# A new static order for one kernel: windowed attention and a channel mix on one core

## Chip, core and metric

One core of a Trainium2 chip. The metric is the device time of one execution in microseconds (us); lower is better. The engines are PE (TensorE: matmuls, with weight loads shown as PEld), DVE (VectorE), ACT (ScalarE), POOL (GpSimd) and SP (SyncE, which here issues nearly all DMAs).

## The reference

Attention over 4 batches of 8 heads, 768 positions and 64 dimensions, in which each position sees the 128 last positions and the first 4 (the sink), followed by a channel mix with three weight matrices:

```python
scores = scale * np.matmul(q, k.transpose(0, 1, 3, 2))
keep = (pos[None, :] < n_sink) | ((rel >= 0) & (rel < window))     # 4 and 128
a = softmax(np.where(keep, scores, -1e9))
x = np.matmul(a, v)                                  # heads side by side: (4, 768, 512)
xk = mu_k * x + (1 - mu_k) * x_prev                  # x_prev: one position earlier
xr = mu_r * x + (1 - mu_r) * x_prev
k = np.maximum(xk @ w_k, 0.0)                        # 512 -> 1024
out = sigmoid(xr @ w_r) * (k * k @ w_v)              # 1024 -> 512
```

All inputs and the output are float32 in HBM; the matmuls run in bf16.

## The kernel before

The work is cut into 12 units of 256 positions: unit u is third u % 3 of batch u // 3. A unit goes through these steps; the names are those of the tiles in the profile, the lines those of the kernel before.

- **Loads** (`load`, lines 284, 294 and 314; `load_weight`, line 330). Q, K and V of a unit come in two DMAs each, of 256 KB. For Q and K of the early units these are 256 pieces of 1 KB, for V (and for Q and K of later units) 1024 pieces of 256 bytes. W_k and W_v come in two DMAs of 1 MB each, W_r in one.
- **Casts to bf16**: `kb<-ks` and `qb<-qs` (lines 512 and 519), `vb<-vs` (617), and the weights `wk_sb`, `wr_sb`, `wv_h` (477, 481, 483).
- **Transposes** of K and Q: on PE into a PSUM bank (547) with a copy out to `kt` or `qt` (560), or, for K from unit 4 and Q from unit 8, by a DMA (534).
- **Attention** (`attend`): scores `sc` on PE (685), their exp `e` on ACT (739), the mask on DVE (753). The four sink positions have their own scores (660), exp `es` (667) and values (727). The value product (772) makes a bank from `e` and `vb`; the DVE takes a reciprocal (786) and writes `x` (789).
- **Mixing** (`mix`): `x` is transposed to `xt` (813, copied out at 822; in the last units by a DMA, 833), DVE forms the difference `td` (841) and eight products of line 852, four `xk` and four `xr`.
- **Channel mix** (`ffn`): key products on PE (903), relu `rl` on ACT or DVE (913, 917), its square `kk` on DVE (925), the gate product (934) with a tanh `th` on ACT (940), the value product `kk` times W_v in two half products (952), the output `ob` on DVE (961) and its store (968).

The order is not left to a run-time or compile-time scheduler. Every step is noted as an operation with a number by `Plan.op`. Three tables at the head of the file decide the rest: `CHOICE` names the engine of those casts, copies and relus that may run on more than one (ACT, DVE, for some POOL), `ORDER` is the one list in which all 1054 operations are emitted, and `SLOTS` gives the buffer of each tile. An engine runs its operations in the order of the list, one behind the other; a step whose operand is late holds up all behind it on its engine. A negative number in `ORDER` is a filler, a product of zeros on PE into a free bank (line 972).

```python
def run(self):
    keys = [(name, key) for o in self.ops for name, key in o["take"]]
    for (name, key), slot in zip(keys, SLOTS, strict=True):
        self.buf[key] = self.pools[name][slot]
    for i in ORDER:
        if i < 0:
            self.fill(self.pools["bank"][-1 - i])
        else:
            self.ops[i]["emit"]()
```

Four PSUM banks serve all products but the scores, which have two double banks of their own. Loads have three buffers each for K, Q, V and the 1 MB weight pieces.

Of the kernel before, what the change touches and what calls it, by code (L numbers as in the profile page):

```python
# [18 lines left out]
    90: "ACT", 92: "ACT", 94: "ACT", 98: "ACT", 100: "DVE", 103: "POOL", 106: "POOL", 111:  # L19
    "DVE", 112: "ACT", 113: "ACT", 139: "DVE", 142: "DVE", 145: "DVE", 148: "DVE", 152: "ACT",  # L20
    161: "DVE", 196: "DVE", 199: "POOL", 202: "DVE", 205: "ACT", 206: "ACT", 223: "DVE", 281:
    "POOL", 283: "DVE", 286: "DVE", 287: "ACT", 288: "DVE", 363: "DVE", 366: "ACT", 367: "ACT",
    438: "POOL", 446: "DVE", 447: "ACT", 449: "DVE", 456: "DVE", 516: "DVE", 518: "DVE", 521:
    "POOL", 526: "ACT", 527: "ACT", 547: "DVE", 605: "ACT", 606: "ACT", 679: "DVE", 684: "DVE",
    761: "ACT", 762: "ACT", 774: "DVE", 832: "DVE", 839: "ACT", 854: "DVE", 862: "DVE", 906:
    "POOL", 910: "DVE", 912: "DVE", 914: "ACT", 915: "ACT", 1004: "DVE", 1028: "DVE", 1036:
    "DVE",
# [15 lines left out]
PAIRS = ()  # L43

VS = ()
# [67 lines left out]
)  # L113

SLOTS = (
# [60 lines left out]
def kernel(  # L176
# [14 lines left out]
    nc = tc.nc  # L191
# [4 lines left out]
    NS = 4  # L196
# [9 lines left out]
    P = Plan()  # L206
# [820 lines left out]
```

## Time and profile before

| what | value |
|---|---|
| median of three runs | 170.79 us (169.55 to 171.17) |
| the profiled execution | 171.36 us |
| its span, first to last instruction | 169.6 us |
| granted TensorE clock | 0.999 |
| PE busy | 158.9 us (94%), 1569 instructions |
| DVE busy | 150.3 us (89%), 393 |
| ACT busy | 126.2 us (74%), 207 |
| POOL busy | 13.0 us (8%), 39 |
| read from HBM, written | 24.12 MB, 6.29 MB |

Busy time is summed per engine from first to last instruction; PE's includes the 32 fillers. A wait of an instruction is put down to the one that released it. Stretches are given in us from the first instruction.

### The profile page before, as it was taken

What the parts mean: (1) busy time and instruction counts of PE and PEld (TensorE: products, weight loads), DVE (VectorE), ACT (ScalarE), POOL (GpSimd) and SP (SyncE); (2) the same over time, 40 slices, a digit from 0 to 9 for tenths busy, and PEclk for the clock granted to TensorE, in tenths of its full rate; (3) what the DMA queues carried; (4) which work ended last, traced back from release to release, by engine and by line L of the source; (5) the groups of instructions that cost most, each with busy time, mean ns of one, the idle gap of its engine ahead of it and who ended that gap; (6) DMA issues with size and microseconds to landing.
All of it is one profiled execution on the core that took longest, in us unless ns stands there. A gap on an engine that the chain in (4) does not pass through costs nothing. (4 is left out here: it accounts for less than half of the span.)

```text
span 169.6 us, 4167 instructions
## 1 busy us (share of the span) xinstructions
PE 158.9 (94%) x1569; PEld 101.4 (60%) x1589; DVE 150.3 (89%) x393; ACT 126.2 (74%) x207; POOL 13.0 (8%) x39
## 2 busy tenths in 40 slices
PE   7997898969999999999999999999999999999991
PEld 2445476734657666767556686674665566664760
DVE  5159999699999999999999999999899999979851
ACT  4379998879997999799979998788658736731230
POOL 7520030001020001000000100000200000000000
PEclk9999999999999999999999999999999999999999
DMA  4999969999999999979969999999996761134303
GB/s 115 289 322 385 249 218 297 332 370 267 226 232 213 159 274 252 269 139 237 196 191 163 202 245 182 205 226 155 223 252 137 190 156 34 63 96 155 124 2 124
DMA packets 79043, 34.61 MB, mean 204 GB/s; under 512 B 67112, under 2 KB 73520, under 8 KB 79024
## 3 DMA queue, kind: packets, MB, share of 16 engines
q1 hardware_dynamic: 79008, 34.35, 87.0%
q8 instruction: 12, 0.20, 0.5%
q14 instruction: 7, 0.06, 0.1%
q10 hardware_dynamic: 16, 0.00, 0.0%
HBM read 24.12 MB, written 6.29 MB: 179 GB/s over the span
## 5 line engine op out<-in xcount | busy, mean ns | idle before, releaser
L903 PE MATMUL bank<-xk,wk_sb 128*128 128x256 bf16 x384 | 51.2, 273 | 0.9 <-DVE xk L852 0.4
L739 ACT ACTIVATE e<-sc 128x1024 bf16<-128x1024 f32 (+1 forms) x48 | 44.9, 961 | 1.7 <-PE sc L685 1.6
L952 PE MATMUL bank<-wv_h,kk 128*128 128x512 bf16 x173 | 44.7, 379 | 0.6
L903 PEld LDWEIGHTS <-wk_sb 128*128 128x128 bf16 x384 | 35.3, 98 | 10.4 <-issue 1.9
L913 ACT ACTIVATE rl<-bank 128x512 bf16<-128x512 f32 x41 | 24.0, 602 | 12.3 <-PE bank L903 7.9
L753 DVE TENSOR_TENSOR e<-e,mask 128x1024 bf16<-128x1024 bf16 (+1 forms) x48 | 30.2, 639 | 1.2 <-ACT e L739 1.0
L952 PEld LDWEIGHTS <-kk 128*128 128x128 bf16 x184 | 17.0, 98 | 16.0 <-DVE kk L925 0.3
L934 PE MATMUL bank<-wr_sb,xr 128*128 128x512 bf16 x87 | 23.5, 379 | 0.6 <-ACT rl L913 0.2
L852 DVE SCALAR_TENSOR_TENSOR xk<-td,mu_all,xt 128x256 bf16<-128x256 bf16 x48 | 22.2, 494 | 0.1
L852 DVE SCALAR_TENSOR_TENSOR xr<-td,mu_all,xt 128x256 bf16<-128x256 bf16 x48 | 22.2, 477 | 0.0
L940 ACT ACTIVATE th<-bank 128x512 f32<-128x512 f32 x24 | 14.5, 606 | 10.3 <-PE bank L934 8.8
L925 DVE TENSOR_TENSOR kk<-rl 128x512 bf16<-128x512 bf16 x48 | 19.4, 416 | 0.5 <-ACT rl L913 0.3
L789 DVE TENSOR_TENSOR x<-bank,rec 128x256 bf16<-128x256 f32 x48 | 19.5, 415 | 0.3
L772 PE MATMUL bank<-vb,e 128*128 128x65 bf16 x352 | 17.3, 194 | 2.3 <-DVE e L753 1.7
L772 PEld LDWEIGHTS <-e 128*128 128x128 bf16 x352 | 14.1, 97 | 6.6 <-DVE e L753 3.0
L961 DVE SCALAR_TENSOR_TENSOR ob<-th,bank 128x512 f32<-128x512 f32 x23 | 15.5, 678 | 1.2 <-PE bank L952 1.1
L934 PEld LDWEIGHTS <-xr 128*128 128x128 bf16 x96 | 9.1, 97 | 9.1 <-issue 0.7
L685 PE MATMUL sc<-qt,kt 64*128 64x128 bf16 (+1 forms) x256 | 13.8, 237 | 0.3 <-ACT kt L560 0.2
L617 ACT CAST vb<-vs 128x512 bf16<-128x512 f32 x18 | 11.3, 630 | 3.0 <-DMA vs<-in_v_dram 3.0
L685 PEld LDWEIGHTS <-kt 64*128 64x128 bf16 x256 | 9.2, 94 | 4.0 <-issue 2.1
L972 PE MATMUL bank<-warm 128*128 128x512 bf16 x32 | 10.1, 457 | 1.2 <-DVE warm L990 1.1
L841 DVE TENSOR_TENSOR td<-xt 128x512 bf16<-128x512 bf16 x24 | 10.0, 428 | 0.2
(71 smaller groups left out, 141.3 us busy)
## 6 DMA issues: line engine op xcount, KB each, us to landing
vs<-in_v_dram SPq DMA_DIRECT2D x24, 256.0 KB, 4.6
qs<-in_q_dram SPq DMA_DIRECT2D x24, 256.0 KB, 5.2
ks<-in_k_dram SPq DMA_DIRECT2D x24, 256.0 KB, 4.6
out_dram<-ob SPq DMA_DIRECT2D x23, 256.0 KB, 2.5
w<-in_moe_w_k_dram SPq DMA_DIRECT2D x2, 1024.0 KB, 9.1
w<-in_moe_w_v_dram SPq DMA_DIRECT2D x2, 1024.0 KB, 11.1
w<-in_moe_w_r_dram SPq DMA_DIRECT2D x1, 1024.0 KB, 7.8
kt<-kb SPq DMA_TRANSPOSE x16, 3.6
```

The costliest lines, as they stand in the source:

```text
L685: nc.tensor.matmul(out=sc[:, a, o0:o1], lhsT=lhs[rows], rhs=rhs[rows], start=u not in BIAS, stop=True, skip_group_check=u in BIAS)
L739: nc.scalar.activation(out=buf[ek][:, :, lo:], in_=buf[sck][:, :, lo:], func=AF.Exp, scale=scale)
L753: nc.vector.tensor_tensor(out=at, in0=at, in1=m, op=ALU.mult)
L772: nc.tensor.matmul(out=o[:, g, a, :], lhsT=e[:, a, e0:e0 + 128], rhs=rhs, start=(T == 0 and i == 0), stop=(i == len(blocks) - 1), skip_gro ...
L789: P.op("DVE", dve(256), lambda ok=ok, rk=rk, c=c: nc.vector.tensor_tensor(out=buf["x", u][:, :, 128 * c:128 * c + 128].rearrange("p g (a d ...
L852: nc.vector.scalar_tensor_tensor(out=buf[key][:, c, :], in0=buf[tk][:, i, :], scalar=mu[w][:, c:c + 1], in1=xt[:, c, t0 - 1:t0 + 255], op0 ...
L903: nc.tensor.matmul(out=ps[:, i, :], lhsT=wk_sb[:, c, 128 * f:128 * f + 128], rhs=xk[:, c, :], start=(c == 0), stop=(c == NC - 1), skip_gro ...
L913: nc.scalar.activation(out=buf[rk], in_=buf[psk].rearrange("p (i t) -> p i t", i=2), func=AF.Relu)
L925: P.op("DVE", dve(512, 0.52), lambda f2=f2, rk=rk: nc.vector.tensor_tensor(out=buf["kk", u][:, 2 * f2:2 * f2 + 2, :], in0=buf[rk], in1=buf ...
L934: nc.tensor.matmul(out=buf[psk], lhsT=buf["xr", u][:, c, 128 * g:128 * g + 128], rhs=wr_sb[:, c, :], start=(c == 0), stop=(c == NC - 1))
L952: nc.tensor.matmul(out=buf[psk], rhs=wv_h[:, f, :], lhsT=buf["kk", u][:, f, 128 * g:128 * g + 128], start=(f == 0), stop=(f == NF - 1))
L961: P.op("DVE", dve(512), lambda psk=psk, tk=tk, bk=bk: nc.vector.scalar_tensor_tensor(out=buf[bk], in0=buf[tk], scalar=1.0, in1=buf[psk], o ...
```

## The change

No operation is added or taken away. The three tables are replaced: 66 operations have another engine, `ORDER` and `SLOTS` are new. Code for two options that both stay empty (`ROWS4` and `BY_ACT`) is added and does nothing. The diff, cut to its core:

```diff
 CHOICE = {
-    90: "ACT", 92: "ACT", 94: "ACT", 98: "ACT", 100: "DVE", 103: "POOL", 106: "POOL", 111:
-    "DVE", 112: "ACT", 113: "ACT", 139: "DVE", 142: "DVE", 145: "DVE", 148: "DVE", 152: "ACT",
...
+    90: "ACT", 91: "ACT", 92: "ACT", 93: "ACT", 95: "ACT", 97: "ACT", 99: "ACT", 100: "POOL",
+    103: "POOL", 106: "DVE", 108: "DVE", 109: "DVE", 139: "POOL", 141: "DVE", 142: "DVE", 144:
...
+ROWS4 = ()
+
+BY_ACT = ()
...
 ORDER = (
-    78, 4, 80, 2, 87, 77, 81, 3, 83, 0, 1, 85, 112, 8, 9, 79, 82, 6, 86, 5, 84, 103, 109, -1,
-    -2, -3, -4, -1, -2, -3, -4, -1, -2, -3, -4, -1, -2, -3, -4, -1, 115, 7, 116, -2, 110, 104,
...
+    4, 79, 77, 80, 0, 78, 81, 1, 82, 85, 2, 3, 8, 83, 6, 7, 84, 112, 9, 86, 19, -1, -2, -3, -4,
+    -1, -2, -3, -4, -1, -2, -3, -4, -1, -2, -3, 115, 5, 100, -4, -2, -3, -4, -2, 101, 88, 102,
...
 SLOTS = (
...
```

What it comes to on each engine:

| operation | before: ACT, DVE, POOL | after: ACT, DVE, POOL |
|---|---|---|
| kb cast | 13, 6, 5 | 14, 5, 5 |
| qb cast | 14, 8, 2 | 11, 8, 5 |
| vb cast | 18, 3, 3 | 13, 5, 6 |
| kt copy | 7, 1, 0 | 6, 2, 0 |
| qt copy | 14, 2, 0 | 15, 1, 0 |
| xt copy | 14, 4, 0 | 15, 3, 0 |
| relu | 41, 7, 0 | 43, 5, 0 |
| W_k, W_r, W_v casts | 4, 6, 0 | 7, 3, 0 |

PE has the same products, with 44 fillers for 32.

**SP's first loads** (unit in figures, halves a and b; q and k halves are 256 KB):

- before: v0a q0a q0b k0a k0b q1a q1b k1a v0b k1b q2a q2b W_k-a W_k-b v1a v1b k2a k2b W_r v2a W_v-a v2b W_v-b q3a k3a q3b k3b q4a q4b k4a v3a q5a v3b k4b
- after: v0a k0a k0b q0a q0b q1a k1a k1b q1b q2a v0b q2b W_k-a k2a W_k-b k2b v1a v1b v2a W_r W_v-b W_v-a v2b q3a k3a k3b q3b q4a q4b q5a q5b k4a v3a v3b k4b

From the 39th of its 132 issues to the 118th the order is the same; of the last fourteen, some stores come earlier.

**POOL's first steps**, after the change: identity, head mask (`hmask`), first window mask (`mask0`), `spread`, vb of unit 0 (first half), sink column, kb and qb of unit 0, kb of unit 1 (first half), vb of unit 0 (second half), window mask, kb of unit 1 (second half), qb of unit 2. Before: window mask, `mask0`, `hmask`, identity, sink column, `spread`, qb and kb of unit 0, sink keys.

**ACT**, from its first copy out of PSUM:

- before: qt0 kt0 kt0 e0 e0 vb0 qt1 e0 e0 kt1 qt1 xt0 e1 e1 kt1 qt2 W_k(0) e1 es1 e1 qt2 rl0 vb1 rl0 W_k(2) kb2 xt1 kt2 xt1
- after: kt0 qt0 e0 qt0 e0 qb1 e0 e0 qb2 qt1 kt1 e1 e1 W_k(1) qt2 qt2 W_k(0) W_k(3) e1 vb1 es1 vb1 e1 rl0 rl0 W_k(2) xt1 kt2 xt1

**DVE** after the change has no cast of W_k any more (it had two); it takes W_r's first half at about the place where W_r's second half stood, and W_v's pieces 2 and 0 behind the two masks of unit 2's first pair, with a V cast of unit 2 between them. From unit 3 on, steps of an engine shift by two to five places on average against each other.

**ACT's first operation** is the small exp that brings the function table; the two DMAs of mu that ACT issues (line 350) come after it and not before.

More of the change, by code (lines that the diff above doesn't have):

```diff
@@ L18 @@
 CHOICE = {
-    90: "ACT", 92: "ACT", 94: "ACT", 98: "ACT", 100: "DVE", 103: "POOL", 106: "POOL", 111:
-    "DVE", 112: "ACT", 113: "ACT", 139: "DVE", 142: "DVE", 145: "DVE", 148: "DVE", 152: "ACT",
[L21 to L27, printed above, removed]
+    90: "ACT", 91: "ACT", 92: "ACT", 93: "ACT", 95: "ACT", 97: "ACT", 99: "ACT", 100: "POOL",
+    103: "POOL", 106: "DVE", 108: "DVE", 109: "DVE", 139: "POOL", 141: "DVE", 142: "DVE", 144:
+    "DVE", 145: "POOL", 151: "ACT", 152: "ACT", 154: "DVE", 161: "DVE", 193: "DVE", 196: "POOL",
+    199: "POOL", 205: "ACT", 206: "DVE", 223: "DVE", 284: "POOL", 287: "DVE", 288: "DVE", 320:
+    "DVE", 363: "DVE", 366: "ACT", 367: "DVE", 438: "DVE", 441: "POOL", 443: "POOL", 447: "ACT",
+    526: "DVE", 527: "ACT", 559: "DVE", 595: "DVE", 602: "DVE", 605: "ACT", 606: "ACT", 677:
+    "DVE", 681: "POOL", 683: "ACT", 684: "ACT", 753: "DVE", 774: "DVE", 830: "DVE", 832: "DVE",
+    838: "ACT", 839: "ACT", 854: "DVE", 908: "DVE", 914: "ACT", 1032: "DVE",
 }
@@ L262, in halves, with walked, block @@
         return slice(2 * half, 2 * half + 2) if u in PAIRS else slice(half, None, 2)
+    def walked(name, u):
+        return name in ROWS4 and by_dma(name, u)
+    def block(name, u, c, g=None):
+        t = buf[name + "t", u]
+        if not walked(name, u):
+            return t[:, c, :, :] if g is None else t[:, c, g, :]
+        t = t.rearrange("p c g t -> p (c g t)").rearrange(
+            "p (h j t w) -> p h w t j", h=2, j=4, w=2)[:, c % 2, c // 2]
+        return t if g is None else t[:, 32 * g:32 * g + 32]
     def by_dma(name, u):
@@ L283, in load @@
                     s0 = 256 * T + 128 * g
-                    P.op("SP", 600.0, lambda key=key, g=g, s0=s0: nc.sync.dma_start(
+                    queue, by = (nc.scalar, "ACT") if f"v{u}" in BY_ACT else (nc.sync, "SP")
+                    P.op(by, 600.0, lambda queue=queue, key=key, g=g, s0=s0: queue.dma_start(
                         out=buf[key][:, g, :, :],
@@ L290, in load @@
             src = {"k": k, "q": q}[name]
-            if by_dma(name, u):
+            if by_dma(name, u) and name not in ROWS4:
                 for g in range(2):
@@ L329, in load_weight @@
         key = ("w32", name, i)
-        P.op("SP", 600.0, lambda: nc.sync.dma_start(out=buf[key], in_=src), rank,
+        queue, by = (nc.scalar, "ACT") if what in BY_ACT else (nc.sync, "SP")
+        P.op(by, 600.0, lambda: queue.dma_start(out=buf[key], in_=src), rank,
              service=2930.0, descs=660, take=[("w32", key)], writes=[(name + "32", i)])
@@ L510, in cast @@
             def cast(copy, raw=raw, rk=rk, hs=hs, half=half, name=name):
-                if by_dma(name, u):
+                if by_dma(name, u) and name not in ROWS4:
                     return lambda: copy(
@@ L528, in prepare @@
                  hold=[raw] + ([rk] if half else []),
-                 reads=([(name, u, half)] if by_dma(name, u) or u in PAIRS else
+                 reads=([(name, u, half)] if by_dma(name, u) and name not in ROWS4 or u in PAIRS else
                         [(name, u, half, w) for w in range(2)]) + ["table"],
@@ L533, in prepare, with turn @@
             if by_dma(name, u):
-                P.op("SP", 1240.0, lambda key=key, rk=rk, half=half: nc.sync.dma_start_transpose(
-                    out=buf[key][:, :, half, :],
-                    in_=buf[rk][:, half, :, :].rearrange("p h d -> p (h d)")), rank + half,
+                def turn(key=key, rk=rk, half=half, name=name):
+                    to = buf[key][:, :, half, :] if name not in ROWS4 else buf[key].rearrange(
+                        "p c g t -> p (c g t)")[:, 512 * half:512 * half + 512].rearrange(
+                            "p (j m) -> p j m", j=4)
+                    nc.sync.dma_start_transpose(
+                        out=to, in_=buf[rk][:, half, :, :].rearrange("p h d -> p (h d)"))
+                P.op("SP", 1240.0, turn, rank + half,
                     service=930.0, descs=512, lag=1300.0, room=1200, reads=[rk + (half,)],
@@ L628, in prepare, with first @@
             return
+        def first(rows):
+            t = buf["kt", u]
+            if not walked("k", u):
+                return t[rows, :, 0, 0:NS]
+            return t.rearrange("p c g t -> p (c g t)").rearrange(
+                "p (h j t w) -> p (w h) t j", h=2, j=4, w=2)[rows, :, 0, :]
         def sink_keys():
@@ L634, in sink_keys @@
                 nc.gpsimd.tensor_copy(out=kz[rows, :, 4 * a:4 * a + NS],
-                                      in_=buf["kt", u][rows, :, 0, 0:NS])
+                                      in_=first(rows))
         P.op("POOL", 500.0, sink_keys, rank + 4, hold=[("kt", u)], port=True,
@@ L661, in sink_scores @@
                                          lhsT=ksink[b % 2][:, 32 * c:32 * c + 32],
-                                         rhs=buf["qt", w][:, c, :, :], start=True, stop=True)
+                                         rhs=block("q", w, c), start=True, stop=True)
             P.op("PE", 150.0 + 109.0 * (len(us) - 1), sink_scores, rank, lag=PE_LAG, mode=2,
@@ L676, in scores @@
             c = chunk(u, k)
-            kt, qt, sc = buf["kt", u], buf["qt", u], buf["sc", u, k]
-            jobs = [(kt[:, c, 0, :], 128, 384, qt[:, c, :, :]),
-                    (kt[:, c, 1, :], 384, 512, qt[:, c, 1, :])]
+            sc = buf["sc", u, k]
+            jobs = [(block("k", u, c, 0), 128, 384, block("q", u, c)),
+                    (block("k", u, c, 1), 384, 512, block("q", u, c, 1))]
             if T > 0:
-                jobs.append((buf["kt", u - 1][:, c, 1, :], 0, 128, qt[:, c, 0, :]))
+                jobs.append((block("k", u - 1, c, 1), 0, 128, block("q", u, c, 0)))
             for (lhs, o0, o1, rhs) in jobs:
@@ L696, in made @@
         def made(name, w, c):
-            if by_dma(name[0], w):
+            if by_dma(name[0], w) and name[0] not in ROWS4:
                 return [(name, w, 0), (name, w, 1)]
```

158 rows, old and new, of tables (ORDER, SLOTS) are left out of this document.

## The prediction

> **What bounds the kernel now.** First the page, for the shares and the DMA row:
>
> ```profile
> span 169.6 us, 4167 instructions
> ...
> PE 158.9 (94%) x1569; PEld 101.4 (60%) x1589; DVE 150.3 (89%) x393; ACT 126.2 (74%) x207; POOL 13.0 (8%) x39
> ...
> DMA  4999969999999999979969999999996761134303
> ```
>
> PE is the bound on the whole, with DVE close behind. A share is a mean over stages, so next the busy times by stretch (PE, PEld, DVE, ACT, POOL, each with its count, then clock, DMA share, GB/s):
>
> ```profile
> 10.00:20.00 10.00, 8.21 (x112) 5.05 (x109) 8.68 (x26) 9.88 (x17) 0.38 (x2) 1.00 1.11 343
> 20.00:30.00 10.00, 9.05 (x109) 6.29 (x109) 9.77 (x27) 9.53 (x17) 1.57 (x2) 1.00 0.81 242
> 30.00:40.00 10.00, 8.29 (x77) 5.45 (x78) 7.95 (x20) 8.14 (x14) 0.00 (x0) 1.00 1.08 346
> 40.00:60.00 20.00, 19.70 (x195) 12.18 (x197) 19.43 (x50) 18.95 (x35) 1.74 (x4) 1.00 1.03 209
> 60.00:110.00 50.00, 49.46 (x551) 33.31 (x558) 49.17 (x130) 45.38 (x75) 1.99 (x6) 1.00 1.08 214
> 110.00:160.00 50.00, 49.59 (x457) 31.71 (x463) 47.63 (x123) 29.17 (x46) 1.22 (x2) 1.00 0.68 147
> ```
>
> From 40 to 160 us PE idles 0.30 + 0.54 + 0.41 = 1.25 us in 120: no order can win more than that there. From 10 to 30 ACT is full. From 30 to 40 all three engines idle about 2 us, so something outside them ends last. The waits of the stretch 18 to 45 us name it, and SyncE's own timeline shows where it comes from:
>
> ```profile
> DVE wv_h L481 <- DMA w<-in_moe_w_v_dram: 1.9, 1, 1.9
> ...
> ACT vb L617 <- DMA vs<-in_v_dram: 1.2, 2, 0.8
> ...
> PE bank L772 <- DVE e L753: 0.9, 1, 0.9
> ```
>
> ```profile
> 10.97 5.53 SPq L284 DMA_DIRECT2D vs<-in_v_dram  x2
> 16.54 5.16 SPq L314 DMA_DIRECT2D ks<-in_k_dram  x2
> ...
> 24.34 2.31 SPq L284 DMA_DIRECT2D vs<-in_v_dram  x1
> 26.76 3.16 SPq L330 DMA_DIRECT2D w<-in_moe_w_v_dram  x1
> ```
>
> An issue takes about 0.6 us here; these took up to 4.8, because loads of V before them had filled the queue. After the second V load of unit 1, K of unit 2 was only accepted at 21.04 us. In the trace's landing times the fastest DMA engine finished that V load at 20.81 and the K load at 23.07, 2.26 us apart where loads of that size follow each other by 0.72 to 0.75: a hole of 1.5 us in the transfers (242 GB/s between 20 and 30 us, 343 before). It makes W_v late, DVE stands at its cast, and the mask of unit 2 behind it keeps PE's value product.
>
> **The change, part by part.** Times are of the profiled execution, 171.36 us: span 169.6 and 1.76 around it. It lies 0.57 above the median of the three runs, 170.79.
>
> *Work moved between engines.* 66 of the casts, copies and relus change engine. By the rows' means DVE loses a net 1 kb (0.42), 1 qt (0.68), 2 relus (1.37), 2 W_k and 1 W_v casts (1.37 + 0.69), 1 xt (0.42) and gains 1 kt (0.69), 2 vb (0.85): 3.4 us less of 150.3. ACT nets +0.6 us, but early: its two more W_k casts are 1.08 each. POOL gets 6 more casts of 0.61 to 0.94.
>
> *What a POOL cast costs DVE.* One td beside a POOL cast took longer than its group's mean of 428 ns:
>
> ```profile
> 41.02 0.67 POOL L519 CAST kb<-ks 128x512 bf16<-128x512 f32 x1 [15.57 <-DMA ks<-in_k_dram]
> ...
> 41.34 0.63 DVE L841 TENSOR_TENSOR td<-xt 128x512 bf16<-128x512 bf16 x1
> ```
>
> That is +0.20. Two products of line 852 beside the POOL cast at 49.44 took 1.23 us, where the pair at 35.53 took 0.88: +0.35. Six casts: 1.2 to 2.1 us, so DVE nets -1.3 to -2.2; I take -1.7. The rule that speaks against this part is in the Trainium skill, SBUF — State Buffer, "SBUF: two separate sides": the port pair of VectorE and GpSimd is an exclusive lock, and the loser blocks for the whole instruction. The trace shows delays on both sides, smaller than a whole cast on DVE's; the rule's own result is the third rival.
>
> *Start, to the first scores.* K of unit 0 is loaded ahead of Q, so it takes Q's landings (5.09 and 5.78 us) and Q takes K's (7.14, 8.73). POOL does its five set-up steps without the window mask (about 4.3 us from 1.28), one V cast and then the K cast, to about 7.0; the Q cast follows at 7.8, transposes (0.24) and ACT's copy (0.59) bring the first scores to about 8.9, from 10.37: 1.5 us earlier.
>
> *Unit 0's values.* The second half of V goes from ninth load to eleventh, landing at about 13.6 (what landed in that slot) instead of 12.13. Its cast moves to POOL (0.62), so the first value product starts at about 14.3, from 12.69: the 1.5 us are gone. Queued behind that cast on POOL are the window mask (0.54) and K's second half of unit 1, ready at about 15.8, from 13.94. On DVE the way from the first reciprocal (13.86 before) to unit 0's last xk (20.50) was 6.64 us; two Q casts (0.73) and a mask (0.62) leave it, one xt copy (0.42) joins, and 0.5 is lost to the late transposes: 5.7 + 0.5 from 14.8 gives 21.0, half a us late.
>
> *Unit 1's exps on ACT.* Between its first kt/qt copy and unit 1's last exp, ACT has six more steps of about 0.5 (start to start) and two W_k casts of 0.95, and five fewer of 0.5: +2.4. It starts 0.5 earlier. Its waits for a landing or for PE were 1.2 us; now it waits for scores, Q's last halves, K's transpose and V of unit 1, which I add up to 2.1. So the last exp ends at 22.22 + 1.9 + 0.9 = 25.0. Behind it are six steps (3.5 us) instead of nine (5.4) up to unit 1's last xt copy: 28.5, from 27.66. With the same 1.9 us of DVE work after it, the last xk of unit 1 is ready at 30.4, from 29.58, and the key products of unit 1 start +0.9 us late. The ends of this term: -0.5 (a third of the early scores survives) and +2.4 (ACT's whole added work is paid). I take +0.9; ACT idles only 0.12 of 10 us in that stretch, so its work passes through.
>
> *The loads of 20 to 38 us.* K of unit 2 now goes ahead of V of unit 1, between the halves of W_k, so the queue holds short loads when the V loads block, and the 1.5 us hole should close. W_r lands at about 28.1 (29.57), W_v's halves at 32.3 and 35.4 (34.16 and 37.89, order swapped), V of unit 2 last at 36.4 (35.17). PE then: key products of unit 1 (8 x 0.43) to 33.85, two gates (1.73) to 35.6, sink values and scores (0.77) to 36.35, a wait for V's cast on DVE to 36.85, two value products (0.5), a gate, half a product, a gate (2.6), a transpose (0.24), half a product (0.86): 41.05. Before, the same work (one half product for one gate) ended at 40.78 + 0.87 = 41.65. Net 0.6 us ahead, so this term alone is -1.5. Its ends: 0 (V of unit 2 or W_v is as late as before) and -1.7 (all of PE's idle in 30 to 40).
>
> *40 us to the end.* SyncE's order is unchanged from its 39th issue to its 118th; PE's and DVE's steps shift by two to five places on average. PE idles 1.25 us there, DVE 3.8, and DVE's work falls by about 1.2 after the start. Ends: -1.0 and +1.5 (a new order can add waits where there were none; the largest single one of DVE on PE was 0.9). I take -0.3.
>
> *Warm-up products.* 32 become 44, all before the first key product, in PE's waits (it idled 1.8 us between 10 and 20 us besides the fillers): nothing, and at most a filler's 0.22 when an operand arrives behind one.
>
> **Sum:** +0.9 - 1.5 - 0.3 = -0.9: 170.46 for an execution like the profiled one, 169.9 for the median.
>
> **Rivals.**
> 1. *The early scores carry through.* If V's late half does not hold unit 0 back by its full 1.5 us, the first term is -0.5; with the hole closed (-1.5) and -0.5 after: 170.79 - 2.5 = 168.3. For it: first scores 1.5 us early. Against: ACT is full from 10 to 30.
> 2. *Slower: V of unit 1 blocks ACT.* On ACT the two casts of unit 1's V now stand ahead of the sink exp and the last exp (before, one was on POOL and the other behind both). If that V lands 1.5 us later than the 23 us I count on, both exps, unit 1's values and its xk wait: the first term is +2.4, and the loads, late too, give back only 0.5: 172.7. It decides from a landing of about 24.5. For it: before, ACT waited 1.2 us for V. Against: nothing else stands between W_k and V than K of unit 2 (1.4 us).
> 3. *POOL takes what DVE gained.* If DVE is blocked for a whole cast (0.65), six cost 3.9 against 3.4 saved: DVE +0.5 and the last term +0.5 instead of -0.3: 170.7. Only two rows bear on it, and both show half or less. It is the Trainium skill's rule above, carried out.
> 4. *New waits after 40 us* of 2 us or more: 172.5. PE's idle of 1.25 leaves little trace of such waits now, but every order after 40 us is new.
>
> **How the numbers follow.** Forecast 0.45 (its own range 169.1 to 171.3), early scores 0.24, V blocks ACT 0.14, POOL 0.09, new waits 0.08. A measurement here can tell about 1% from no change, 169.1 to 172.5. Faster by over 1%: 0.24 and a few hundredths of the forecast, 0.27. Slower: 0.14 and half of 0.08, and a little of POOL, 0.20. Same: 0.53. The range goes to the low rival and the slow one: 168.0 to 172.7.
>
> **What would show it.** Right: first exp near 9, first value product near 14.3, no issue of K behind a V load longer than 2 us, DVE's wait for W_v gone, PE busy in 30 to 40 us above 9. Wrong: last exp of unit 1 before 23 or after 26.5; more than 2 us of PE idle from 40 to 160 us.

## The result, and the profile after

| | before | after |
|---|---|---|
| median | 170.11 us (168.92 to 172.31, 10 runs) | 172.28 us (170.98 to 174.07, 10 runs) |
| the profiled execution | 171.36 us | 171.27 us |

The ratio is 1.011 [1.0076, 1.0145]: slower by about 1.9 us, where 0.9 us less was forecast. (Ratios leave disturbed runs out, so they can differ from the quotient of two medians.) The two profiled executions don't show it: before's lies 1.25 us above its median, after's 1.0 below its own. What follows therefore uses several executions of each start.

The page of after, the lines that answer to those shown of before:

```profile
span 169.5 us, 4191 instructions
...
PE 159.6 (94%) x1583; PEld 102.3 (60%) x1601; DVE 148.3 (88%) x388; ACT 126.0 (74%) x206; POOL 18.5 (11%) x45
...
DMA  4999989999989998979995999999996894122303
```

DVE has 2.0 us less work and POOL 5.5 more. Busy times by stretch of after (PE, PEld, DVE, ACT, POOL, each with its count, then clock, DMA share, GB/s):

```profile
10.00:20.00 10.00, 8.85 (x117) 5.77 (x116) 8.34 (x23) 9.19 (x15) 3.73 (x8) 1.00 1.10 353
20.00:30.00 10.00, 8.75 (x110) 5.76 (x108) 9.58 (x26) 9.56 (x16) 1.10 (x1) 1.00 0.98 263
30.00:40.00 10.00, 9.85 (x90) 6.43 (x92) 9.96 (x25) 10.00 (x16) 0.61 (x1) 1.00 1.08 341
40.00:60.00 20.00, 19.83 (x200) 12.36 (x201) 19.58 (x51) 19.17 (x36) 1.88 (x5) 1.00 1.06 208
60.00:110.00 50.00, 48.64 (x549) 33.36 (x554) 47.44 (x128) 43.87 (x74) 2.79 (x5) 1.00 1.05 207
110.00:160.00 50.00, 49.02 (x457) 31.46 (x462) 46.61 (x118) 29.74 (x49) 2.11 (x4) 1.00 0.75 154
```

The idle time of 30 to 40 us is gone, on all three engines. From 40 to 160 us PE idles 0.17 + 1.36 + 0.98 = 2.5 us instead of 1.25. Before 20 us PE's busy time holds twelve more fillers, so a higher figure there is not more progress. The longest waits of after from 18 to 45 us, and SyncE's timeline:

```profile
POOL qb L535 <- DMA qs<-in_q_dram: 18.8, 2, 16.0
POOL kb L535 <- DMA ks<-in_k_dram: 5.6, 1, 5.6
PEld L755 <- issue: 1.2, 3, 0.4
PEld L931 <- ACT wk_sb L493: 0.9, 2, 0.7
```

```profile
10.20 1.30 SPq L329 DMA_DIRECT2D ks<-in_k_dram  x1
...
12.36 1.47 SPq L329 DMA_DIRECT2D ks<-in_k_dram  x1
13.88 7.97 SPq L299 DMA_DIRECT2D vs<-in_v_dram  x3
21.89 0.78 SPq L346 DMA_DIRECT2D w<-in_moe_w_r_dram  x1
22.79 5.03 SPq L346 DMA_DIRECT2D w<-in_moe_w_v_dram  x2
```

No wait of DVE or ACT for W_v or V is left, and no issue of K takes longer than 1.47 us. In this execution the loads did what was predicted. The start of after, from the timeline (start, length, instruction, idle time before it):

```profile
7.89 0.43 DVE L535 CAST qb<-qs 128x512 bf16<-128x512 f32 x1 [4.47 <-DMA qs<-in_q_dram]
7.92 0.87 POOL L535 CAST qb<-qs 128x512 bf16<-128x512 f32 x1 [0.88 <-DMA qs<-in_q_dram]
...
8.17 1.25 PE L1000 MATMUL bank<-warm 128*128 128x512 bf16 x5
...
8.23 0.83 DVE L535 CAST kb<-ks 128x512 bf16<-128x512 f32 x1
...
9.26 0.39 PE L568 MATMUL bank<-ident,qb 128*128 128x128 bf16 x4
9.48 0.81 PE L1000 MATMUL bank<-warm 128*128 128x512 bf16 x3
9.68 0.59 ACT L581 COPY qt<-bank 128x512 bf16<-128x512 bf16 x1 [0.98 <-PE bank L568]
...
10.32 0.51 PE L713 MATMUL sc<-qt,kt 64*128 64x256 bf16 x8
```

The first scores start at 10.32 us, not at 8.9: K is early, but Q's cast on POOL ends at 8.79, five fillers (L1000) are still ahead of its transposes at 9.26, and three more precede the scores.

Where the executions stand, in us. "First value product" and "unit u" are taken at a first weight load, that of the value products and that of unit u's key products; W_v is the landing of the half that comes first and of the one that comes last.

| execution | first value product | unit 0 | unit 1 | unit 2 | from 1 to 2 | W_v | its time |
|---|---|---|---|---|---|---|---|
| before | 12.69 | 20.16 | 28.51 | 51.42 | 22.91 | 34.16, 37.89 | 171.36 |
| before_again | 12.72 | 20.19 | 28.66 | 50.69 | 22.03 | 33.54, 37.29 | 171.33 |
| after | 13.87 | 21.47 | 30.48 | 50.43 | 19.95 | 32.16, 35.00 | 171.27 |
| after_again | 14.35 | 21.95 | 30.96 | 50.90 | 19.94 | 32.70, 36.33 | 171.93 |

So the new start is 1.8 to 2.5 us late when unit 1's key products begin, and in these executions wins 2.1 to 3.0 back by unit 2. The two executions of before are slow ones for their kernel: two other old starts below (old_to_63, old_k2_early), whose medians equal before's, begin unit 2 at 49.47 and 49.73.

### The profile page after: what moved, and what is told of

Read it like the earlier page. It is cut to its first block, busy times and chain, and to the rows that moved or that the text cites. A ratio compares the mean times of both kernels' runs of the same rounds, so it can differ in the third digit from the quotient of the medians.

```text
span 169.5 us, 4191 instructions
## 1 busy us (share of the span) xinstructions
PE 159.6 (94%) x1583; PEld 102.3 (60%) x1601; DVE 148.3 (88%) x388; ACT 126.0 (74%) x206; POOL 18.5 (11%) x45
## 4 chain that ended last, share of the span: by engine, by line
PE 59%; ACT 15%; DMA 11%; DVE 10%; issue 2%; SPq 1%; DVEq 0%; ACTq 0%
PE bank L931 16%; PE bank L980 16%; PE bank L962 8%; DMA ks<-in_k_dram 6%; PE bank L1000 5%; PE bank L800 4%; ACT e L767 4%; PE sc L713 4%; DMA vs<-in_v_dram 3%; DMA qt<-qb 2%; ACT qt L581 2%; ACT wk_sb L493 2%; PE bank L841 2%; DVE xk L880 2%; ACT rl L941 2%
## 5 line engine op out<-in xcount | busy, mean ns | idle before, releaser
L931 PE MATMUL bank<-xk,wk_sb 128*128 128x256 bf16 x384 | 49.7, 273 | 0.3 <-ACT wk_sb L493 0.2
L941 ACT ACTIVATE rl<-bank 128x512 bf16<-128x512 f32 x43 | 25.2, 608 | 20.4 <-PE bank L931 18.5
L880 DVE SCALAR_TENSOR_TENSOR xr<-td,mu_all,xt 128x256 bf16<-128x256 bf16 x48 | 22.7, 484 | 0.0
L880 DVE SCALAR_TENSOR_TENSOR xk<-td,mu_all,xt 128x256 bf16<-128x256 bf16 x48 | 21.7, 477 | 0.2
L800 PEld LDWEIGHTS <-e 128*128 128x128 bf16 x352 | 14.8, 97 | 5.1 <-DVE e L781 1.0
L1000 PE MATMUL bank<-warm 128*128 128x512 bf16 x44 | 12.9, 435 | 1.1 <-DVE warm L1018 1.1
L638 POOL CAST vb<-vs 128x512 bf16<-128x512 f32 x6 | 4.8, 798 | 65.1 <-DMA vs<-in_v_dram 39.3
L869 DVE TENSOR_TENSOR td<-xt 128x512 bf16<-128x512 bf16 x24 | 10.5, 439 | 0.8 <-DMA xt<-x 0.5
```

The costliest lines, as they stand in the source:

```text
L800: nc.tensor.matmul(out=o[:, g, a, :], lhsT=e[:, a, e0:e0 + 128], rhs=rhs, start=(T == 0 and i == 0), stop=(i == len(blocks) - 1), skip_gro ...
L880: nc.vector.scalar_tensor_tensor(out=buf[key][:, c, :], in0=buf[tk][:, i, :], scalar=mu[w][:, c:c + 1], in1=xt[:, c, t0 - 1:t0 + 255], op0 ...
L931: nc.tensor.matmul(out=ps[:, i, :], lhsT=wk_sb[:, c, 128 * f:128 * f + 128], rhs=xk[:, c, :], start=(c == 0), stop=(c == NC - 1), skip_gro ...
L941: nc.scalar.activation(out=buf[rk], in_=buf[psk].rearrange("p (i t) -> p i t", i=2), func=AF.Relu)
L1000: P.fill = lambda bank: nc.tensor.matmul(out=bank, lhsT=warm[:, 0:128], start=True, rhs=warm.unsqueeze(1).to_broadcast([128, 2, 256]), sto ...
```

## Experiments

**A second profile of each kernel** (no edit), before_again and after_again:

> The kernel before, profiled once more, since its first profiled execution (171.36 us) lay 1.25 above its median. Theory 1 (the new order loses from 60 us on, where it uses loads as they land): an execution near 170 us, PE idle from 40 to 160 us again near 1.2 us, and the 1 us it gains on the first profile lies before 60 us. Theory 2 (the loss is in the start): the start of this execution is up to 1 us quicker than in the first profile, and so is every later step.

> The changed kernel, profiled once more, since its first profiled execution (171.27 us) lay 1.0 below its median of 172.28. Theory 1: its start up to 60 us as in the first profile within 0.5 us, and 2 to 4 us of PE idle from 60 to 140 us, by other loads than the first time. Theory 2: unit 1's exps later than the 25 us of the first profile and no recovery by 40 us.

Measured: 171.33 and 171.93 us, one execution each, the second and the fourth line of the table. PE idles 0.8 us from 40 to 160 us in before_again and 1.6 in after_again.

**Halves of the order.** Operations are emitted in the one order up to a seam and in the other behind it. In early_new and late_new the seam is at operation 403 (about 63 us) and all buffers are given out anew; in new_to_63 and old_to_63 the seam is the same and each tile keeps its own order's buffer, renamed where the two meet; new_to_131 has its seam at about 131 us. The rule by which the lists are joined, in short (the engines of the operations follow their part):

```diff
-ORDER = BEFORE
+ORDER = AFTER[:403] + [op for op in BEFORE if not in AFTER[:403]]    # new_to_63
+ORDER = BEFORE[:403] + [op for op in AFTER if not in BEFORE[:403]]   # old_to_63
```

> The new orders and engines for the first 403 operations (up to about 60 us), the old ones for the rest; buffers given out anew. Theory 1: no slower than the kernel before, 169.5 to 170.3 us (ratio 0.996 to 1.001). Theory 2: the whole loss, about 172 us (ratio 1.01). A loss spread over both parts: about 171 (1.005).

> The old orders and engines for the first 403 operations, the new ones for the rest. Theory 1: the whole loss or a little more, 172 to 173 us (ratio 1.011 to 1.016). Theory 2: like the kernel before, 170 us (ratio 1.00). A loss spread over both: about 171 (1.005).

> The new orders, engines and buffers for the first 403 operations (up to about 63 us), then the old ones, with each old buffer number mapped to the buffer that holds the same tile at the seam, so that old buffers follow each other as before. The two hybrids before lost 7 to 8 us all along after the seam, where buffers had been given out anew. Theory 1 (the loss lies after 60 us): 169.5 to 170.5 us, ratio 0.995 to 1.001. Theory 2 (it lies in the start): ratio 1.01. Spread over both: 1.005.

> The old orders for the first 403 operations, then the new ones, buffers mapped at the seam. Theory 1: ratio 1.011 to 1.016. Theory 2: 1.00. Spread over both: 1.005.

> The new orders for the first 886 operations (up to about 132 us), then the old ones, buffers mapped at the seam. Theory 1, with the loss between 63 and 131 us: ratio 1.01, 172 us. If it lies in the last 35 us: 170 us, ratio 1.00.

| kernel | median us | ratio to before | unit 1 | unit 2 |
|---|---|---|---|---|
| early_new | 178.50 | 1.047 [1.0423, 1.0518] | 30.34 | 50.28 |
| late_new | 177.11 | 1.0396 [1.0345, 1.0447] | 28.48 | 50.45 |
| new_to_63 | 172.18 | 1.0099 [1.0066, 1.0133] | 31.18 | 51.11 |
| old_to_63 | 170.47 | 0.9992 [0.9961, 1.0024] | 28.69 | 49.47 |
| new_to_131 | 171.89 | 1.0063 [1.0028, 1.0099] | 31.47 | 51.39 |

The first two say nothing of the orders, but something of the buffers: early_new has the order and the engines of new_to_63, and late_new those of old_to_63, and only the buffer numbers differ; that alone makes them 6 to 7 us slower. With the buffers kept the answer is plain: the new order's first 63 us bring the whole loss, and its remaining 107 us behind the old start neither cost nor win more than 0.4%. The same profile also shows what the second term of the prediction rested on. The old start of old_to_63, with the old loads, in its stretch from 30 to 40 us:

```profile
30.00:40.00 10.00, 9.80 (x89) 6.16 (x87) 9.88 (x23) 9.99 (x17) 0.73 (x1) 1.00 1.12 323
```

PE is busy 9.80 there, against 8.29 in the execution that the prediction read, 8.84 in before_again and 9.02 in late_new, which has the same start. W_v landed at 31.03 instead of 34.16, 33.54 and 33.17, with the same order of loads. The hole in PE is no fixed amount: it was largest in the execution that was read, and in one of four it is absent.

**Casts taken off POOL** (few_pool): seven casts of units 5, 8, 9 and 11 go back to ACT (six) and DVE (one).

```diff
 CHOICE = {
-    441: "POOL", 443: "POOL", 681: "POOL", ...
+    441: "ACT", 443: "ACT", 446: "DVE", 681: "ACT", 761: "ACT", 762: "ACT", 915: "ACT", ...
```

> The changed kernel with seven casts of units 5, 8, 9 and 11 taken from POOL back to the engines that had them (six to ACT, one to DVE), orders else unchanged. If POOL's casts hold DVE up: 1 to 2 us faster than the changed kernel, 170.5 to 171.3 (ratio 1.000 to 1.006). Theory 1: POOL's in-order waits for loads matter little, 172 us (1.01).

Measured 175.85 us, 1.0253 [1.0184, 1.0321]. The casts are better on POOL in this order: on ACT one of them waits 2.05 us for its Q to land, a tanh stands behind it, PE waits 3.2 us for that tanh, and from 85.2 to 88.5 us the granted clock is 0.50. The rival by which POOL takes what DVE gained falls as to the late units; this run says nothing of POOL's casts in the start.

**The fillers ahead of the first scores** (no_fill):

```diff
 ORDER = ( ... 115, 5, 100,
-    -4, -2, -3, -4, -2,
     101, 88, 102, 20, 103, 109, 10, 106,
-    -4, -4, -4, -4, -2,
     104, 105,
-    -2, -2, -2,
     117, ...
```

> The changed kernel without the 13 fillers that stand in TensorE's queue between the start product and the first score product; nothing else is changed. Theory F (fillers ahead of unit 0's transposes cost the new start its time): the first score product goes from 10.2-10.7 us (four executions of the new start) to about 9.0, unit 1's first key product from 30.5-31.5 to 29-30, ratio to the kernel before 0.998-1.004. Theory S (the order of the loads costs it: V's late half lands at 13.3 instead of 12.1): the first scores may come early, but the first value product stays at 13.9 or later and unit 1's key product at 30.5 or later, ratio 1.007-1.013. Theory C (the casts given to ScalarE cost it): the same as theory S here. If the granted clock falls for want of fillers, ratio above 1.013.

Measured 171.79 us, 1.0031 [0.9989, 1.0073]. The first scores start at 10.05, only 0.3 earlier, behind Q's cast on POOL; unit 1 is at 31.18, no earlier than with the fillers. How much of the loss is gone can't be told: the interval allows all of it, while the median lies 0.8% above the 170.50 of before beside it. And the run does more than it was meant to: without these fillers the granted clock of 10 to 20 us falls to 0.83. It gives no support to theory F, and does not exclude it cleanly.

**The order of the loads alone**, both ways: new_sp_old is after with the old order of SyncE's first 29 loads, old_sp_new is before with the new one.

```diff
-    4, 0, 1, 2, 3, 8, 6, 7, 9, 19, 5, 20, 10, 17, 11, 18, 12, 13, 21, 14, 16, 15, 22, ...
+    4, 2, 3, 0, 1, 8, 9, 6, 5, 7, 19, 20, 10, 11, 12, 13, 17, 18, 14, 21, 15, 22, 16, ...   # new_sp_old
```

> The changed kernel with the order of SyncE's first 29 loads (to about 60 us) as in the kernel before; the compute engines' orders and the casts' engines are those of the changed kernel. Theory S (the order of the loads costs the 1%): V's late half lands near 12.1 again, unit 1's first key product comes at 28.5-29.5 and the ratio to the kernel before is 0.996-1.004. Theories F and C: landings as in the kernel before, yet unit 1's first key product stays at 30 or later, ratio 1.006 or more. The new orders were found for the new loads, so above 1.013 would say only that the two orders don't fit.

> The kernel before with the changed kernel's order of SyncE's first 29 loads; orders of the compute engines and the casts' engines are those of the kernel before. It is the prediction's second term by itself: by it TensorE's busy time in 30-40 us goes to 9.8 or more (8.29, 8.84 and 9.80 in three executions of the old start), and the ratio is 0.991-0.997 if the first twelve loads cost nothing. Theory S: V's late half lands at 13.3, unit 1's first key product at 30 or later instead of 28.5-28.7, ratio 1.006-1.013. Theories F and C: the key product stays within 0.7 us of 28.6, ratio 0.993-1.003.

Measured 180.40 us, 1.0584 [1.0538, 1.0630], and 173.98 us, 1.0236 [1.0190, 1.0283]. Each set of compute orders wants its own loads; for one, the halves of W_v come in the order in which they are not cast. Up to unit 1 they can be read: the new loads under the old orders put unit 1 at 30.00 instead of 28.6, the old loads under the new orders at 32.90. So the loads are not a part that could be kept or undone by itself.

**Two casts of W_k back on DVE** (wk_dve):

```diff
 CHOICE = {
-    90: "ACT", 91: "ACT", 92: "ACT", 93: "ACT", ...
+    90: "ACT", 92: "ACT", ...
```

> The changed kernel with two of the four casts of W_k (quarters 1 and 3) back on VectorE, where the kernel before has them; nothing else is changed. Theory C (ScalarE, which has all four of them ahead of unit 1's exponentials, is what makes unit 1 late): the last exponential of unit 1 ends 1-2 us earlier than 25.5-26.5, its key products start near 29.5, ratio 0.998-1.004. Theories F and S: the loss stands, ratio 1.007-1.013; VectorE's copies of the transposed operands of unit 1 come later, so up to 1.016.

Measured 173.69 us, 1.0186 [1.0144, 1.0229], unit 1 at 32.73. What theory C expected did not come: relieving ACT at DVE's expense makes unit 1 1.2 to 2.2 us later. The run shows that DVE has no room for these casts; it does not show what ACT alone would give.

**A seam at about 34 us** (195 operations): new_to_34 and old_to_34, made like new_to_63.

> The changed kernel's orders, cast engines and buffers for the first 195 operations (about 34 us: units 0 and 1 up to unit 1's key products and the casts of the weights begun), the kernel before's from there, buffers mapped at the seam. Theory E (all of the loss is there by unit 1's key products): unit 1's first key product at 30.5-31.5 us, ratio to the kernel before 1.005-1.013. Rival M (the loss is made between 34 and 60 us, the early lateness is caught up): ratio 0.997-1.003.

> The mirror of it: the kernel before's first 195 operations, the changed kernel's from there. Theory E: unit 1's first key product at 28.5-28.7, the changed orders after it start from there, ratio 0.993-1.001, and TensorE's stretch from unit 1's to unit 2's first key product as in the old starts (20.8-22.9 us). Rival M: ratio 1.005 or more.

Measured 174.63 us, 1.0254 [1.0201, 1.0308], unit 1 at 31.48, and 174.39 us, 1.0109 [1.0017, 1.0201], unit 1 at 28.36, then PE busy only 6.12 of 30 to 40 us. Inconclusive: the seam lies among the W_v casts, and both lose behind it.

**V's late half of unit 0 earlier** (v_early):

```diff
-    4, 0, 1, 2, 3, 8, 6, 7, 9, 19, 5, 20,
+    4, 0, 1, 2, 3, 8, 6, 7, 5, 9, 19, 20,
```

> The changed kernel with one load moved: the late half of unit 0's V goes from eleventh to ninth place in SyncE's order, ahead of Q's late half of unit 1 and Q of unit 2; nothing else is changed. Theory V (that landing holds up unit 0's values and so all behind): it lands near 11.5-12 instead of 13.2-13.4, the first value product starts 0.8-1.2 earlier than 13.9-14.6, unit 1's first key product at 29.3-30.2, ratio 1.000-1.006. Rival A (the orders on ScalarE and VectorE of unit 0's second head hold it: its first exponential stood at 12.0-12.5 before any V was needed): the landing comes early, the first value product stays within 0.4 of before, unit 1's key product at 30.4 or later, ratio 1.007-1.013.

Measured 172.90 us, 1.0131 [1.0075, 1.0187]. It lands at 11.83 instead of 13.29 and is cast by 12.49, yet the first value product starts at 14.66 and unit 1 at 31.28. So the early landing by itself does not bring unit 0 forward. The move is not free, though: Q's late half of unit 1 now lands at 12.56 instead of 11.39, and DVE waits 0.35 us for it ahead of unit 0's masks.

**K of unit 2 ahead of V of unit 1, in the old order** (old_k2_early), the prediction's second term alone:

```diff
-    10, 11, 12, 13, 17, 18, 14,
+    10, 17, 11, 18, 12, 13, 14,
```

> The kernel before with one thing of the changed loads: K of unit 2 goes ahead of V of unit 1, between the halves of W_k. It is the prediction's second term by itself. By the prediction: the hole in the transfers near 21-23 us closes, W_v's first half lands near 32 instead of 34.2, TensorE is busy 9.5 or more of 30-40 us, ratio 0.990-0.995. Rival L (the weights' lateness of the profiled execution was that execution's own: in two others of the same start they landed at 33.5 and 31.0): W_v's first half lands anywhere in 31-34, ratio 0.997-1.003; if V of unit 1, now behind K of unit 2, holds up unit 1's values, 1.003-1.010.

Measured 170.50 us, 0.9993 [0.9961, 1.0026]. The profiled execution has

```profile
20.00:30.00 10.00, 9.04 (x109) 6.19 (x108) 9.99 (x27) 9.41 (x17) 1.16 (x2) 1.00 1.05 292
30.00:40.00 10.00, 9.68 (x87) 6.25 (x88) 9.88 (x24) 9.99 (x16) 0.86 (x1) 1.00 1.13 326
```

The hole closes, PE is nearly full in 30 to 40, and the median is the same. By the interval the term is worth between -0.7 and +0.4 us, not -1.5.

**V early and 20 fillers less** (v_early_bare): v_early's loads, no_fill's edit, and seven more fillers out.

```diff
     134, 113, 144, 129, 87, 89, 141,
-    -1, -1, -1, -1,
     120, ... 114, 146, 127, 13, 147, 130,
-    -1,
     153, ... 171, 155,
-    -2, -2,
     136, ...
```

> The changed kernel with the late half of unit 0's V in ninth place among the loads and without the 20 fillers that follow the start product up to 18 us (13 ahead of the first scores, 4 ahead of the first value product, 3 in unit 1's transposes); 24 fillers are left. Each of the two edits alone did not bring unit 1 forward (key product at 31.2 and 31.3 us). Theory K (each hides behind the other: with V late the fillers are free, with the fillers there V's landing is): first value product near 13.3 instead of 13.9-14.9, unit 0's first key product near 20.7-21.2 instead of 21.5-22.5, unit 1's at 29.3-30.3, ratio 0.998-1.006. Theory D (ScalarE's queue sets it: it stands idle to 8.2 us, then has one piece of work after the other, and the cast of W_k's quarter 0 ends at 21.4-22.4): the value product comes early, unit 0's key product stays at 21.4 or later, unit 1's at 30.5 or later, ratio 1.006-1.014.

Measured 171.97 us, 1.0135 [1.0067, 1.0203]. Its stretch from 10 to 20 us:

```profile
10.00:20.00 10.00, 8.66 (x92) 6.35 (x90) 7.13 (x20) 7.59 (x12) 3.72 (x8) 0.50 1.08 360
```

The granted clock falls to 0.50; four transposes (10.46 us) take 0.61 us for 0.40 in after, and the first value product stays at 14.47. Theory K is not shown, and not cleanly excluded either, since the edit changed the clock as well.

**One W_k cast from ACT to POOL** (wk1_pool):

```diff
-    91: "ACT",
+    91: "POOL",
```

> The changed kernel with one cast, quarter 1 of W_k, moved from ScalarE to GpSimd, which stands idle from about 16 to 22 us; nothing else is changed. Theory D: ScalarE's queue moves up by the cast's 1.08 us, the cast of quarter 0 ends at 20.3-21.3, unit 0's first key product comes 0.6-1.0 us earlier (20.6-21.5), unit 1's last exponential at 24.5-25.5, unit 1's first key product at 29.5-30.5, ratio 1.001-1.008. Theory K: unit 0's key product stays at 21.4 or later and the loss stands, ratio 1.008-1.014; if the cast on GpSimd slows VectorE beside it, up to 1.016.

Measured 172.10 us, 1.0101 [1.0060, 1.0142]. ACT did move up: W_k's quarter 0 is cast by 20.84 instead of 21.3 to 22.5. Unit 1 stays at 31.17 (30.3 to 31.6 in the other new starts), so theory D's gain did not come. But the cast that left ACT holds DVE up from POOL:

```profile
17.42 1.30 POOL L473 CAST wk_sb<-w 128x1024 bf16<-128x1024 f32 x1 [0.54 <-DMA w<-in_moe_w_k_dram]
...
17.83 1.17 DVE L831 TENSOR_TENSOR td<-xt 128x512 bf16<-128x512 bf16 x1
```

A `td` takes 0.42 us by itself; this one ends 0.28 us behind the cast and costs DVE 0.75. So both W_k runs took work off ACT and gave time to DVE, and neither relieves ACT alone.

**What is left: DVE's queue, level with ACT's.** This reading rests on the profiles; no run was made to test it. The last exponential of unit 1 on ACT and the last mask of unit 1 on DVE, in before, after and wk1_pool:

```profile
21.13 1.09 ACT L739 ACTIVATE e<-sc 128x1024 bf16<-128x1024 f32 x1
...
24.32 0.66 DVE L753 TENSOR_TENSOR e<-e,mask 128x1024 bf16<-128x1024 bf16 x1
```

```profile
24.45 1.06 ACT L767 ACTIVATE e<-sc 128x1024 bf16<-128x1024 f32 x1
...
25.54 0.69 DVE L781 TENSOR_TENSOR e<-e,mask 128x1024 bf16<-128x1024 bf16 x1
```

```profile
24.45 1.03 ACT L729 ACTIVATE e<-sc 128x1024 bf16<-128x1024 f32 x1
...
26.45 0.68 DVE L743 TENSOR_TENSOR e<-e,mask 128x1024 bf16<-128x1024 bf16 x1
```

Before, that mask starts 2.1 us after the exponential has ended (2.10 to 2.23 in seven old starts): ACT is ahead, DVE comes last. In after it starts 0.03 us behind, and 0.03 to 0.21 in the ten other new starts in which the casts of W_k stay on ACT: ACT has used up its lead, its exponential ends 3.3 us later and DVE's mask starts 1.2 us later. In wk1_pool ACT is 0.98 us ahead again, and the mask comes no earlier. So in the new start both queues end together at this point, and work taken off ACT can win no more than DVE allows.

What DVE allows: take DVE from its last idle time over 0.3 us up to the end of unit 1's last `xk`. Before, that is 11.6 to 29.6 us:

```profile
11.60:29.60 18.00, 15.58 (x203) 10.42 (x202) 17.62 (x50) 17.41 (x29) 1.57 (x2) 1.00 0.94 291
```

After, 11.3 to 31.3 us:

```profile
11.30:31.30 20.00, 17.55 (x217) 11.43 (x216) 19.14 (x51) 19.34 (x31) 4.28 (x9) 1.00 1.02 307
```

DVE starts 0.3 us earlier and ends 1.7 later: it has 19.14 us of work for 17.62, +1.5, and 0.5 us more of small gaps. Without any gap, its work from 11.26 on would still end only at 30.40, 0.8 us later than before's 29.58, whatever ACT does. The rest of the 1.7 us lies in gaps, some of which are waits behind ACT. ACT too is nearly full (19.34 of 20.0), so the share cannot say which of the two ends last. The stretches of the two W_k runs:

```profile
11.60:31.90 20.30, 17.86 (x218) 11.49 (x216) 19.99 (x51) 18.56 (x30) 5.11 (x10) 1.00 1.01 312
```

```profile
12.20:33.50 21.30, 18.18 (x218) 11.21 (x216) 20.88 (x53) 17.79 (x29) 3.83 (x8) 1.00 0.99 309
```

The first is wk1_pool: ACT has slack (18.56 of 20.30) and the stretch is as long as ever. The second is wk_dve: two casts more on DVE, the stretch 21.30, ACT at 17.79. In seven old starts (before, before_again, late_new, old_to_63, old_to_34, old_k2_early, old_sp_new) the stretch is 17.98 to 18.38 us, in seven new ones whose start is unedited (after, after_again, early_new, new_to_63, new_to_131, few_pool, new_to_34) 20.02 to 20.55. It begins at 11.05 to 11.91 (13.09 in old_sp_new, whose unit 1 is late by about as much) and at 11.12 to 12.04.

What the work is, by groups. Before:

```profile
L483 DVE CAST wk_sb<-w 128x1024 bf16<-128x1024 f32 x2 | 1.4, 684 | 0.0
...
L519 DVE CAST qb<-qs 128x512 bf16<-128x512 f32 x3 | 1.2, 412 | 0.0
...
L519 DVE CAST kb<-ks 128x512 bf16<-128x512 f32 x2 | 0.8, 419 | 0.0
```

After:

```profile
L880 DVE SCALAR_TENSOR_TENSOR xr<-td,mu_all,xt 128x256 bf16<-128x256 bf16 x3 | 1.4, 477 | 0.0
L581 DVE COPY kt<-bank 128x512 bf16<-128x512 bf16 x2 | 1.4, 684 | 2.2 <-PE bank L568 2.2
...
L850 DVE COPY xt<-bank 128x512 bf16<-128x512 bf16 x2 | 0.8, 425 | 0.3 <-PE bank L841 0.2
L672 DVE TENSOR_TENSOR vsink<-bank,hmask 128x512 bf16<-128x512 f32 x1 | 0.7, 687 | 0.0
...
L581 DVE COPY qt<-bank 128x512 bf16<-128x512 bf16 x1 | 0.7, 684 | 0.0
```

Out of the stretch went two W_k casts (1.4) and two `qb` and one `kb` cast (1.2): 2.6 us. Into it came two `kt` and one `qt` copy (2.1; before, ACT made these copies), the sink values' mask `vsink` (0.7, which ran at 7.4 us before, in DVE's idle time), one `xt` copy (0.4) and one `xr` (0.5): 3.7. That is +1.1 of the 1.5. The other 0.4 is lost overlap: instructions that stand close together on DVE overlap a little, and in after they do so by 3.1 us in all, before by 3.5. The 2.2 in the `kt` row is an idle time just before the stretch, and `vsink` stands behind it. No run here took work off DVE in the new start, so that this would repair it is not shown.

## Why the prediction was wrong, step by step

- **Start, to the first scores: wrong.** 8.9 predicted, 10.2 to 11.1 in seven new starts, 10.37 before. Q's cast was to be done on POOL by about 7.8; its load landed at 7.79, and the cast, beside two on DVE, took 0.87 and ended at 8.79. The fillers were priced at nothing; the 13 ahead of the scores, taken away, gave back 0.3.
- **Unit 0's values: right in time (14.3; 13.7 to 15.0), the reason not borne out.** V's landing was to hold them; in v_early it came 1.5 us earlier and they did not. Unit 0's last `xk`, put at 21.0, ended at 21.3 to 22.9.
- **Unit 1's exps on ACT, +0.9: the step that failed.** It took ACT alone as the queue that ends last and left DVE's as it was. The last exponential came at 25.4 to 26.6 (25.0 predicted) and the last `xk` at 31.1 to 32.4 (30.4), so the term measures +1.6 to +2.8. In after, half a us of the miss lies ahead of the last exponential; another half lies in the six steps behind it, which took 4.0 us for 3.5 because ACT waited twice for transposes of `x`, which DVE writes; the last 1.9 us were right (1.8). In place of ACT alone the profiles show two queues that end together, DVE's with 1.5 us more work and 0.5 more of gaps.
- **Work moved between engines:** DVE's total fell by 2.0 (1.7 predicted), which was right and misled: in the stretch that counts it rose by 1.5. The total was not divided by stage.
- **What a POOL cast costs DVE: the size was right, the reading of it not.** In the start of after, the Q cast on POOL took 0.87 us for its usual 0.61, and DVE's second cast beside it 0.83 for 0.43. DVE's cast ends 0.27 us after POOL's (9.06 and 8.79); the `td` that the prediction shows ends 0.28 after its cast (41.97 and 41.69), and the `td` of wk1_pool 0.28 (19.00 and 18.72). The Trainium skill, SBUF — State Buffer, section "SBUF: two separate sides", says that the shared port goes to one of the two for its whole instruction; the trace agrees: DVE finishes a fixed time after the POOL cast, so it loses what is left of that cast when it starts, and not a whole one. Instructions that read PSUM beside a POOL cast keep their length (`x` at 15.21 in after: 0.42 us). In the profile of after five DVE instructions lose 1.7 us in all, in that of before three lose 1.0: far from the 3.9 of the third rival.
- **The loads of 20 to 38 us, -1.5: the second step that failed.** In the profiled execution the landings were right within 0.8 us (W_r 28.83, W_v 32.16 and 35.00, V of unit 2 36.13) and PE's hole closed. But the hole was entered at the size of one execution, and as time won at the end. Over four executions of the old start W_v moves by 3 us and PE's busy time from 8.29 to 9.80, and by itself the edit, which closes the hole, is worth -0.7 to +0.4; why the end does not see the closed hole was not settled. The stretch from unit 1 to unit 2 is 20.8 us in old_to_63 and old_k2_early, whose W_v lands by 31.5, 22.0 to 22.9 in before, before_again and late_new, and 19.9 in new starts. So against an old start without the hole the new one wins back 0.9 us of its 1.4 to 2.9: its unit 2 begins at 50.3 to 51.5, theirs at 49.47 and 49.73. With +1.6 to +2.8 for the first term and about nothing for this one the prediction's sum gives +1.3 to +2.5; measured was +1.9.
- **40 us to the end, -0.3:** neutral by old_to_63, within its bounds. The sign named for an error there, more than 2 us of PE idle, did show in after (2.5), but not in after_again (1.6) or old_to_63 (1.1). One new wait, of PE for ACT's tanh near 82 us, stands in the profile of after, and ahead of it on ACT a cast that waits for its load:

```profile
PE bank L841 <- ACT th L968: 1.0, 1, 1.0
```

```profile
78.73 0.62 ACT L528 CAST kb<-ks 128x512 bf16<-128x512 f32 x1 [1.41 <-DMA ks<-in_k_dram]
```

The two go together: ACT waits 0.96, 1.41, 1.55 and 2.11 us for that K in wk1_pool, after, after_again and v_early, and PE 0.5, 1.0, 1.1 and 1.7 for the tanh. Both are absent from old_to_63, which has the same late order behind the old start. There SyncE issues the K at 71.79 and it lands at 74.69; in after it is issued 1.8 us later, at 73.61, and lands 4.0 later, at 78.70. Why the transfer itself takes longer was not tried. How the rest of the loss divides among the stages behind unit 2 differs from one execution to the next and was not settled.
- **The rivals.** "V of unit 1 blocks ACT" gave a time near the result (172.7), but that V landed at 23.7, before the 24.5 from which it decides. POOL's rival is contradicted by few_pool and by the rows above, the late waits' by old_to_63; the early scores did not come.

## What to carry to other kernels

When a change moves work between engines, sum each engine's queue between two milestones, not over the whole kernel: here DVE's total fell by 2.0 us and its work ahead of unit 1's last operand rose by 1.5. Where two engines are both nearly full, the share of busy time does not tell which one ends last; measure how far one is ahead of the other where they meet, and when a piece of work is taken off one of them, see that the other does not pay for it. And a stall that is to be repaired should be read from more than one execution, and repaired by itself, before it is entered at its full size: here closing it alone won nothing at the end.

## What the runs showed of the hardware that was not expected

With 20 of the 44 fillers out, the granted clock of 10 to 20 us fell to 0.50, and with 13 out to 0.83, against 1.00. The Trainium skill, TensorE: Matmul & The Clock Gate, "Part 1: The HAM clock gate", says that the clock halves after an idle window of about 3.4 us; the 0.50 agrees, but no such idle time is in the trace: with 20 fillers out PE was busy 1.78 of the 3.4 us from 6.5 to 9.9, with no gap longer than 0.94, and the clock was 0.50 from then to 20.1. Fillers in PE's waits, which the prediction entered at nothing, held the clock. The first half of W_v, with the same loads ahead of it, landed at 31.0, 33.2, 33.5 and 34.2 us in four executions.
